# Attention solve and state products in fp32 without operand splits, with changed planner costs and offsets, in a fused attention and two-MoE kernel

## The chip, the cores and the metric

The kernel runs on one core of one Trainium2 chip. The metric is device time in microseconds (us); the median of several executions counts. A profile of one execution shows each engine: PE (TensorE matmuls; PEld is its weight loads), DVE (VectorE), ACT (ScalarE), POOL (GpSimd) and SP, which issues the DMAs.

## What is computed

A linear attention with a state of 40 x 40 per head (batch 4, 8 heads, 768 steps), then two feed-forward layers over its output, 3072 tokens of width 320 and 2048 hidden units:

```python
for t in range(S):
    y[:, :, t] = np.einsum('bhd,bhde->bhe', rt, state)
    Sa = np.einsum('bhde,bhe->bhd', state, at)
    state_decay = state * wt[:, :, None, :] - np.einsum('bhd,bhe->bhde', Sa, bt)
    state = state_decay + np.einsum('bhd,bhe->bhde', vt, kt)
x = attn_out.transpose(0, 2, 1, 3).reshape(B * S, H * D)
h = x @ w_in;    x = (h * np.cos(h)) @ w_out                        # first MoE
h = x @ w_in2;   out = (h * np.clip(h + 3, 0, 6) / 6) @ w_out2      # second MoE
```

## The kernel before, in words

The 768 steps are cut into 12 chunks of 64. A unit is one chunk of one batch entry, all 8 heads: 48 units. All matmuls of the MoE take f16 operands, each number split into a high and a low f16 part, and three products (high-high, high-low, low-high) are added in PSUM. The attention does the same with its operands before the change.

The functions of a unit, in order: `pA` loads a, r, b, k (tile `raw`) and the decays (`pip`); `pB` multiplies them and splits the result into `KBs` and `ARs`; `pT` transposes these by DMA into `KBT` and `ART`; `pC` multiplies them and masks the result (`LN`), whose upper 64 rows are split into `NT`; `pL` stores the lower 64 rows to DRAM. Per chunk, `iL` to `iE` solve 32 triangular systems: `iB` does 31 steps of two DVE instructions, `iC` and `iC1` split the result `Th` and write it through DRAM into `TT` and `Lt`, `iD` and `iE` fill the remaining block with fp32 matmuls (PSUM tile `q`). Then, per unit again: `cL` and `cV` load v and split it into `FS`; `cU` makes the right-hand side u (products of the state `ST` and of `NT` with `FS`), split into `uh` and `uls` (in `S8a`); `cA` applies the solution `TT` to u and splits the result into the lower rows of `FS`; `cAT` transposes `FS` by DMA into `FT`; `cG` multiplies it with `ART`, masks the result (`gm`) and splits it into the two `GF` tiles; `cF` makes output rows and the new state from `GF`, `E` (a copy of `KBs`) and `Srep` in one PSUM tile; `cS` decays the state `S8a`; `cST` transposes it by DMA; `cXT` transposes the output rows into `x1T`. PSUM tiles of cU, cA, cG and cF share one ring of two (`t`).

The MoE (`mA`, `mB`) runs per chunk in eight steps of two hidden blocks each: 256 matmuls into `h` for both layers together, ACT and DVE make the nonlinearity in `s` and split it into `ghl`, and 192 matmuls go into `acc`. The first MoE of a chunk needs the output rows `x1T` of that chunk's four units.

The order is not the program's. The class `Plan` records every instruction with a cost, a list scheduler replays them with a model of engines and DMA, and emits in the order that it finds; `TUNE` holds an offset of priority for each function and instruction, `SLACK`, `AHEAD` and `MARGIN` hold limits of the scheduler, `T_C` and `D_C` say at what due time a chunk's units are recorded and how far apart. An operation recorded on `either` goes to DVE or POOL, a copy to DVE or ACT, as the scheduler chooses. All compute is recorded by one helper, so nearly all rows of the profile have line L419 (L415 for copies that the scheduler put on ACT): tile names tell them apart. All DMAs but two are issued in SP's queue.

Of the kernel before, what the change touches and what calls it, by code (L numbers as in the profile page):

```python
# [43 lines left out]
T_P, D_P, T_I, D_I, T_C, D_C, T_M2, T_WM, LAG = 48.0, 2.0, 36.0, 7.0, 26.05, 2.1, 8, 150, 2  # L44
# [4 lines left out]
    "decay_const": (406, -4, -216, 2, (69, -5)),  # L49
    "decay0": (0, 509, 274, 0, (1, 42, -5, -44, -13, -34, -127, -64, -11, 116, -48, -99, 17, -40, -43, 12, -192,  # L50
        -141, -67, -15, -3, 6, -4, 32, -39, -1, -6, -10, 7, 22, -66, -28, -2, -6, 10, -7, -48)),
    "consts": (97, -153, -168, 11, (-19, 91, 1, -32, -33, 38, 4, -23, 79, 145, -9, 10, -75, 14, 4, 6, 11, -12, -35)),
    "consts1": (-254, 100, 347, 0, (-14,)),
    "consts2": (60, 417, 197, 0, (-11, -4, -48)),
    "pA": (0, 51, -99, 0, (-1, 41)),
    "pB": (0, -16, -1, 39, (0, 0, -1, 0, 0, 0, 1)),
    "pT": (-1, 70, -30, 0, (2,)),
    "pC": (-20, -1, -45, 0, (0, 2, -8, 14)),
    "pL": (1, 5, 467, 0, (-1,)),
    "rest": (124, -153, -38, 17, (-10, -2)),  # L60
    "dsq0": (-68, 293, -36, 0, (18,)),
    "chunk_decay": (-5, 51, -56, 118, (-27, 37, 3, 51)),
    "iL": (2, 22, -1287, 19, (-27, 0, -88, 35)),
    "iA": (61, -507, 208, 0, (-7, -5, -31, -12, 139)),
    "iB": (0, 0, 0, 0, (-3,)),
    "cL": (-1, 110, -26, 13, (6,)),
    "iC": (-7, -28, 23, 4, (-1, -26, -32, -81, 0, -14, 0, -10)),
    "iC1": (-4, -59, -2, 0, (89, 12, -13, -75, 13, -72, -11, -157)),
    "iD": (2, 577, 43, 51, (0, -1)),
    "cV": (1, -46, 12, 6, (-7, -3, 1)),  # L70
    "iE": (-209, 177, -297, 0, (-83, -39, 22)),
    "cU": (0, -1, -193, 0, (4, 0, -1)),
    "cA": (0, 17, -2, 0, (0, -53, 1, 3)),
    "cAT": (-74, 88, -241, 0, (-60,)),
    "cD": (-18, 7, -10, 82, (-13,)),
    "cG": (-2, -8, 9, 21, (-28, 0, -11, -7, 20, -2)),
    "cF": (-13, 1, 0, 173, (-19, 0, 0, 6, 4, 4, 6, 0, 0, -3)),
    "cXT": (-45, -151, 140, 0, (1,)),
    "cST": (5, -4, -19, 35, (2, 2, -5, -2)),
    "ld_w0": (173, -410, -126, 30, (-10,)),  # L80
    "prep_w0": (-22, 276, 9, 0, (-4, -11, 0, -2, -8, -15)),
    "decay1": (-11, 149, -9, 0, (34, 172, -8, 22, 15, -25, 42, 35, -39, 258, -75, -41, -47, -2, -30, -30, -20, -15,
        -5, 1, 0, 27, -12, -44, -6, 150, 248, 12, -9, 19, -14, -101, 9, -13, -6, -87, -23, -31)),
    "dsq1": (346, 63, -151, 0, ()),
    "decay2": (0, 274, -154, 112, (54, 240, -12, 6, 1, 0, -8, -5, 0, 38, -28, 146, -22, 23, -8, 0, -68, -32, -17,
        -7, -18, 2, 0, -52, -1, 0, 38, -19, 0, -15, 18, 6, -12, -64, -23, -31, -52, 17)),
    "cS": (-20, 1, -253, 85, (24,)),
    "dsq2": (-106, -198, -1, 0, (11,)),
    "ld_w1": (-21, 475, 315, 0, ()),
    "prep_w1": (-8, 423, 309, 0, (2, 0, -20, 0, 28, 0, 7)),  # L90
    "mA0": (0, 0, 0, 0, (0, 3, 0, 0, 12)),
    "mB0": (2, 0, 2, 0, (0, 0, 0, 0, 14, 3, 174, 12, 19, -114, 0, -170, -24, 44)),
    "mT": (373, -89, -145, 287, (-14,)),
    "mA1": (0, 8, 11, 165, (0, 26)),
    "mB1": (6, 0, 0, 0, (0, 0, 0, 5, 93, -96)),
    "mO": (-15, -533, -33, 0, (0, -4)),
    "wmax0": (-50, 365, 603, 74, (-17,)),
    "wmax1": (-49, 1, -147, 82, (4,)),
    "wcol": (-50, 302, -353, 190, (-20, -7, 0, -170, 60, -60, 105)),
    "flags": (153, -38, 4, 0, (-83, -72, 51, 21, 31, -14, 76, 60, 30, -72, 81, -15, -68, -54, -25, 111, -3, -24,  # L100
        -19, 131, -91, -99, 96, -71, 64, -111)),
# [3 lines left out]
SLACK, AHEAD, MARGIN = [132, 0, 20, 0, 383], [0, 150, 70, 54], [422, 48, 296, 22]  # L105
RING = {"raw": 2560, "KBT": 2048, "LN": 2048, "v": 1280, "uh": 640, "FT": 2048, "gm": 2048, "pd": 2560, "xy": 1280,
        "wst": 2048, "wx": 1024, "s": 2048, "xs2": 1536, "ghl": 2048, "E": 1280, "ART": 2048, "NT": 1152}
# [28 lines left out]
POOL_GAIN = 0.25  # L136
# [3 lines left out]
class Plan:  # L140
# [9 lines left out]
    def cover(self, ap):  # L150
# [6 lines left out]
        key = (off, tuple(dims), es)  # L157
# [51 lines left out]
    def rec(self, attr, eng, name, a, kw):  # L209
# [10 lines left out]
        if name.startswith("dma"):  # L220
# [6 lines left out]
            if name == "dma_start":  # L227
                run = _run(outs[0], ins[0])
                dma = by / 360.0 * (2 if run < 512 else 1)
            else:  # L230
                r, w = ins[0].shape[0], by // 2 // ins[0].shape[0]
                dma = w / 128 * 112 * r / 128
                c = 1244.0 if r == 128 and w >= 1024 else 1175.0
        elif eng == "PE":
            c = max(n / 2.4 + 2.5, 28.0)
            shape = tuple(32 if x <= 32 else 64 if x <= 64 else 128 for x in (ins[0].shape[0], _free(ins[0])))
        elif eng in ("DVE", "ANY"):
            c = 70 + n * 1.042
            es = max(mybir.dt.size(x.dtype) for x in outs + ins)
            if name == "tensor_copy":  # L240
                c = 70 + n * (0.26 if es == 2 else 0.52)
            elif name == "tensor_scalar":
                c = 70 + n * 0.52
            elif name == "reciprocal":
                c = 70 + n * 6.3
            if any(_free(x) == 1 for x in ins):
                c += 60
# [20 lines left out]
        else:  # L268
            o = dict(eng=eng, c=c, alt=cp if eng in ALTS else None, dma=dma, deps=set(), prio=self.prio, calls=[],
                     grp=(self.group, outs[0].tensor.name), i=i, port=False, shape=FULL)  # L270
# [4 lines left out]

            o["port"] = name not in ("memset", "tensor_reduce", "reciprocal") and all(getattr(x.tensor, "_space", None) != PSUM for x in ins)
# [6 lines left out]
    def order(self):  # L283
# [38 lines left out]
        start = [0] * n  # L322
        gone = set()
# [38 lines left out]
        while evs:  # L362
# [14 lines left out]
            for e in sorted(touched):  # L377
# [7 lines left out]
                if e < 4 and AHEAD[e] > 0:  # L385
                    lim = 100 * t + c * AHEAD[e]
                    if any(100 * ready_t[u] < lim and pr[u] < pr[i] - 400 * MARGIN[e] for u in soon[e]):
                        continue
                gone.add(i)
# [36 lines left out]
def label(g):  # L426
# [7 lines left out]
    elif ev[0] in "pc" and ev in ("pA", "pB", "pT", "pC", "pL", "cL", "cV", "cU", "cA", "cAT", "cD", "cG", "cS", "cF", "cXT", "cST"):  # L434
# [14 lines left out]
def _free(ap):  # L449
# [3 lines left out]
    return n  # L453

# [15 lines left out]
def kernel(  # L470
# [43 lines left out]
    cvec = big.tile([128, 4], F32, name="cvec")  # L514
# [5 lines left out]
    for nm, k in (("x", NU), ("o1", 2 * NC), ("dec", 2 * NG), ("raw", NU), ("fs", NU), ("T", 2 * NC), ("wc", 16),  # L520
# [7 lines left out]
    TTp = big.tile([128, NH * C + 64], F16, name="TT")  # L528
    TT = TTp[:, 0:NH * C].rearrange("p (h t) -> p h t", h=NH)
    FSs = [big.tile([128, H, 128], F16, name=f"FS{i}") for i in range(2)]  # L530
    GFt = [big.tile([128, H * (C + D) + 24], F16, name=f"GF{i}") for i in range(2)]
    GFh, GFl = (t[:, 0:H * (C + D)].rearrange("p (h e) -> p h e", h=H) for t in GFt)
# [6 lines left out]
    uls = S8a[0:64, 384:544].bitcast(F16).rearrange("p (h e) -> p h e", h=H)  # L539
# [5 lines left out]
    tmp = big.tile([128, 136], F32, name="tmp")  # L545
# [10 lines left out]
    Tm = [dr.tile([64, NH, 32], F32, name=f"Tm{i}") for i in range(2)]  # L556
    Thl = [dr.tile([2, C, NH, C], F16, name=f"Thl{i}") for i in range(2)]
# [26 lines left out]
    def square(src, p0, p1_, n, nm, i, o=None):  # L584
# [3 lines left out]
        if len(src.shape) == 3:  # L588
            o = o.rearrange("p (a b) -> p a b", b=src.shape[2])
# [3 lines left out]
    def consts():  # L593
        nc.sync.dma_start(out=mskL, in_=cst[0])
        nc.sync.dma_start(out=mskG, in_=cst[1])
# [873 lines left out]
```

## Time and profile before

| | us |
|---|---|
| median of 3 runs | 1272.9 (1268.25 to 1284.62) |
| the profiled execution | 1271.3 |
| its span, first to last instruction | 1269.4 |
| DVE busy in it | 1067.0 (84%) |
| PE busy | 910.1 (72%) |
| ACT busy | 792.8 (62%) |
| POOL busy | 180.4 (14%) |

Busy time is the union of an engine's instructions. A matmul row lasts from its start to its modelled end and overlaps the next ones, so the distance between two starts, not the row's length, tells what PE spends on one. Idle time of an engine counts only where the engine sets the end.

### The profile page before, as it was taken

The numbers are of one execution on the slowest core, as the hardware profiler recorded it, in microseconds if no ns is written. First come the engines' busy times: TensorE is split into PE (matmuls) and PEld (weight loads), VectorE is DVE, ScalarE is ACT, GpSimd is POOL, SyncE is SP. The second block draws the span as 40 slices with busy tenths as digits, with TensorE's granted clock in tenths as the row PEclk, the third lists the DMA queues.
The fourth block names the chain that finished last, engine by engine and source line by source line (L and its number), as shares of the span: only waits on it lengthen the run. The fifth ranks groups of instructions, "written<-read, shape, count | busy, mean of one in ns | idle before, by whom it ended". The sixth has DMA issues, their size and how long they took to land.

```text
span 1269.4 us, 29683 instructions
## 1 busy us (share of the span) xinstructions
PE 910.1 (72%) x11378; PEld 732.8 (58%) x11378; DVE 1067.0 (84%) x2434; ACT 792.8 (62%) x1642; POOL 180.4 (14%) x206
## 2 busy tenths in 40 slices
PE   0010033571668889699899898988999899999995
PEld 0000023561457668577777676766777777778874
DVE  8999999889989988869989799698796997967543
ACT  1664358485678667657676577686766866645352
POOL 2322111123423110101000010010120100100000
PEclk9999999795679899789999899899898999999998
DMA  6997478775787584776767748868477674532010
GB/s 204 244 186 177 107 225 151 159 162 124 149 171 148 108 156 102 134 144 103 130 143 135 142 83 151 148 113 155 103 126 150 115 134 93 94 63 46 11 24 14
DMA packets 474362, 162.65 MB, mean 128 GB/s; under 512 B 446789, under 2 KB 456049, under 8 KB 473826
## 3 DMA queue, kind: packets, MB, share of 16 engines
q1 hardware_dynamic: 473922, 160.00, 62.6%
q8 instruction: 91, 1.49, 0.5%
q10 hardware_dynamic: 288, 0.67, 0.2%
q14 instruction: 61, 0.50, 0.1%
HBM read 80.10 MB, written 25.61 MB: 83 GB/s over the span
## 4 chain that ended last, share of the span: by engine, by line
DVE 42%; PE 23%; DMA 11%; ACT 8%; issue 6%; SPq 3%; POOL 0%; DVEq 0%; ACTq 0%; POOLq 0%
PE acc L419 9%; PE h L419 8%; DVE Tt L419 6%; DVE tmp L419 5%; DVE S8a L419 4%; DVE ghl L419 4%; DVE wout L419 4%; PE q L419 4%; DVE s L419 3%; SPq L419 3%; DMA Lt<-Tm 2%; DVE win L419 2%; PE t L419 2%; DVE FS L419 2%; DVE GF L419 2%
## 5 line engine op out<-in xcount | busy, mean ns | idle before, releaser
L419 PE MATMUL acc<-wout,ghl 128*128 128x320 f16 x2304 | 371.8, 309 | 36.7 <-DVE ghl L419 29.6
L419 PEld LDWEIGHTS <-win 128*128 128x128 f16 x3328 | 312.1, 101 | 74.3 <-issue 27.6
L419 PEld LDWEIGHTS <-ghl 128*128 128x128 f16 x2304 | 217.1, 100 | 122.2 <-DVE ghl L419 35.1
L419 PE MATMUL h<-x1T,win 128*128 128x256 f16 (+1 forms) x1664 | 192.9, 275 | 25.4 <-DVE s L419 17.5
L419 ACT ACTIVATE s<-h,cvec 128x512 f32<-128x512 f32 x192 | 130.4, 680 | 119.4 <-PE h L419 81.8
L419 PE MATMUL h<-x2T,win 128*128 128x256 f16 (+1 forms) x1664 | 187.0, 267 | 0.0
L419 DVE TENSOR_TENSOR ghl<-s,ghl 128x512 f16<-128x512 f32 x182 | 127.6, 703 | 8.7 <-ACT ghl L415 5.2
L419 PE MATMUL p<-ART,KBT 120*128 120x64 f16 x384 | 21.4, 204 | 124.1 <-DMA ART<-ARs 73.7
L419 DVE TENSOR_TENSOR tmp<-Tt,Lt 128x126 f32<-128x126 f32 (+22 forms) x372 | 104.9, 282 | 6.5 <-DMA Lt<-Ls 3.3
L419 DVE TENSOR_TENSOR Tt<-Tt,tmp 128x126 f32<-128x126 f32 (+22 forms) x372 | 103.6, 279 | 3.6
L415 ACT ACTIVATE ghl<-s 128x512 f16<-128x512 f32 x127 | 79.3, 625 | 34.7 <-DVE s L419 27.3
L419 DVE SCALAR_TENSOR_TENSOR s<-h,s 128x512 f32<-128x512 f32 x96 | 65.7, 686 | 38.0 <-ACT s L419 37.5
L419 DVE SCALAR_TENSOR_TENSOR s<-s,h 128x512 f32<-128x512 f32 x96 | 65.2, 680 | 33.6 <-ACT s L419 33.2
L419 PEld LDWEIGHTS <-KBT 120*128 120x128 f16 x384 | 18.7, 104 | 127.7 <-DMA KBT<-KBs 84.7
L419 PE MATMUL t<-E,GF 128*128 128x40 f16 x1152 | 46.1, 184 | 40.1 <-DVE GF L419 32.3
L419 PE MATMUL q<-Lt,Tt 32*32 32x32 f32 x768 | 32.9, 203 | 49.3 <-DMA Lt<-Tm 49.3
L419 PEld LDWEIGHTS <-GF 128*128 128x128 f16 x1152 | 38.7, 99 | 49.1 <-DVE GF L419 34.5
L419 POOL TENSOR_TENSOR wout<-wout 128x512 int32<-128x512 int32 (+1 forms) x28 | 50.2, 1802 | 103.4 <-ACT wout L419 73.2
L419 PEld LDWEIGHTS q<-Lt,Tt 32*32 32x32 f32 x768 | 30.1, 118 | 53.5 <-issue 35.9
L419 PE MATMUL t<-FS,NT 128*128 128x40 f16 x768 | 36.7, 183 | 22.2 <-DVE FS L419 12.4
L419 POOL TENSOR_TENSOR S8a<-S8a,pd 40x320 f32<-40x320 f32 x23 | 25.7, 1123 | 176.0 <-DMA pd<-Ds 175.6
L419 PEld LDWEIGHTS <-ART 120*64 120x64 f16 (+1 forms) x704 | 43.9, 106 | 6.7 <-issue 4.4
(157 smaller groups left out, 1764.1 us busy)
## 6 DMA issues: line engine op xcount, KB each, us to landing
raw<-in_arbk_dram SPq DMA_DIRECT2D x46, 320.0 KB
v<-in_vv_dram SPq DMA_DIRECT2D x96, 80.0 KB
pip<-Dec SPq DMA_DIRECT2D x46, 160.0 KB
wout<-in_moe_w_in_dram SPq DMA_DIRECT2D x12, 512.0 KB
Ls<-LN SPq DMA_DIRECT2D x48, 128.0 KB
Lt<-Ls SPq DMA_DIRECT2D x48, 128.0 KB
TT<-Thl SPq DMA_DIRECT2D x12, 512.0 KB
wstat<-in_moe_w_out_dram SPq DMA_DIRECT2D x10, 512.0 KB
```

The lines of the kernel that those rows point to most:

```text
L415: self.nc.scalar.activation(func=AF.Copy, **kw)
L419: getattr(getattr(self.nc, attr), name)(*a, **kw)
```

## The change

The two f16 parts of an operand are dropped in four places, and the products take fp32 tiles: in `cU` the masked `LN` (now kept in six buffers, its lower half no longer stored as `NT`) with v; in `cA` the solution `TT` (fp32, two halves of 64 partitions) with `u32`; in `cF` the masked result and the vectors in `GFs` (fp32, two buffers) with `E`, which holds the product `bk` itself. v is loaded straight into `GFs`, and one cast and one subtraction over 128 rows make `FS` after `cA`. The products of `cU` with the state use only the first 64 columns of `ART`. `pB` makes its product in two instructions, and the upper decay rows come by a DMA in `pA` instead of a copy. The solve stores fp32 (`Tf`, two DMAs instead of four; `Tm` only half). Scaling by the decay and the split of the state work on pairs of units. In the planner, a key of its overlap cache has the partition count too, DMAs, fp32 matmuls, scans and operands at another start partition get other costs, `D_C` goes from 2.1 to 3.8, and all offsets are new.

```diff
-T_P, D_P, T_I, D_I, T_C, D_C, T_M2, T_WM, LAG = 48.0, 2.0, 36.0, 7.0, 26.05, 2.1, 8, 150, 2
+T_P, D_P, T_I, D_I, T_C, D_C, T_M2, T_WM, LAG = 48.0, 2.0, 36.0, 7.0, 26.05, 3.8, 8, 150, 2
...
-                dma = by / 360.0 * (2 if run < 512 else 1)
+                run = min(run, 20480)
+                dma = by / run * (9 + run * 0.045) / 16
...
+            if ins[0].dtype == F32:
+                c = max(4 * n / 2.4, 40.0 + 0.6 * _free(ins[0]))
...
+                if e in (1, 2):
+                    c, was[e] = c + max(o["off"], was[e]), o["off"]
...
         ldq.dma_start(out=pip[0:64].rearrange("p h x e -> p h (x e)"), in_=dec(n).rearrange("h t x e -> t h (x e)"))
+        ldq.dma_start(out=pip[64:128, :, 1], in_=dec(n)[:, :, 1].rearrange("h t e -> t h e"))
...
-        nc.either.tensor_copy(out=pip[64:128, :, 1], in_=pip[0:64, :, 1])
-        rf = raw.rearrange("p h x e -> p (h x e)")
-        nc.either.tensor_tensor(out=rf, in0=rf, in1=pip.rearrange("p h x e -> p (h x e)"), op=ALU.mult)
+        bk = E_t[n] = pE.tile([128, H, D], F32, tag="E", name="E")
+        nc.either.tensor_tensor(out=bk, in0=raw[:, :, 1], in1=pip[:, :, 1], op=ALU.mult)
+        nc.either.tensor_tensor(out=raw[:, :, 0], in0=raw[:, :, 0], in1=pip[:, :, 0], op=ALU.mult)
...
-        E_t[n] = pE.tile([128, H, 2 * D], F16, tag="E", name="E")
-        nc.either.tensor_copy(out=E_t[n], in_=kb[:, :, 0:2 * D])
...
-        ntp = pN.tile([128, H * C + 64], F16, tag="NT", name="NT")
-        nt = ntp[:, 0:H * C].rearrange("p (h t) -> p h t", h=H)
-        nc.either.tensor_copy(out=nt[64:128], in_=ln[64:128])
-        dp("nt", E_NT).tensor_tensor(out=nt[0:64], in0=ln[64:128], in1=nt[64:128], op=ALU.subtract)
...
-        nc.sync.dma_start(out=Tm[i][0:32].rearrange("(t k) h s -> (k h) t s", k=2), in_=Tn)
-        nc.sync.dma_start(out=Tm[i][32:64].rearrange("(a r) h t -> (r h) a t", r=2), in_=Th[64:128])
-        nc.sync.dma_start(out=TM, in_=Tm[i])
-        nc.sync.dma_start(out=TT, in_=Thl[i].rearrange("x s h t -> (x s) h t"))
+            nc.sync.dma_start(out=Tf[i][32 * k:32 * k + 32, :, 32 * k:32 * k + 32].rearrange("(a r) h t -> (r h) a t", r=2),
+                              in_=Th[64 * k:64 * k + 64])
+        nc.sync.dma_start(out=Tm[i].rearrange("(t k) h s -> (k h) t s", k=2), in_=Tn)
+        nc.sync.dma_start(out=TM[0:32], in_=Tm[i])
+        nc.sync.dma_start(out=TM[32:64], in_=Tf[i][32:64, :, 32:64])
+        for g in range(2):
+            nc.sync.dma_start(out=TT[64 * g:64 * g + 64], in_=Tf[i][:, 16 * g:16 * g + 16])
...
-        nc.vector.scalar_tensor_tensor(out=TT[64:96, hs, 32:64], in0=qv[32:64], scalar=ISC, in1=TT[0:32, hs, 32:64],
-                                       op0=ALU.mult, op1=ALU.subtract)
...
-        ldq.dma_start(out=v[64:128], in_=vv[n])
-        ldq.dma_start(out=v[0:64], in_=vv[n])
-        V_t[n] = v
+        ldq.dma_start(out=GFs[n % 2][64:128, :, C:C + D], in_=hde(vv[n]))
...
+        if c > 0:
+            for h in range(H):
+                nc.tensor.matmul(uv[:, h, :], art[:120, h, 0:C], stt[:120, h, 0:D], start=(h == 0), stop=False)
         for h in range(H):
-            w = nt[:, h * C:h * C + 128]
-            if c > 0:
-                nc.tensor.matmul(uv[:, h, :], art[:120, h, :], stt[:120, h, 0:D], start=True, stop=False)
-            nc.tensor.matmul(uv[:, h, :], w, fs[:, h, 0:40], start=(c == 0), stop=False)
-            nc.tensor.matmul(uv[:, h, :], w, fs[:, h, 40:80], start=False, stop=True)
...
+            nc.tensor.matmul(uv[:, h, :], ln[64:128, h, :], gf[64:128, h, C:C + D], start=(c == 0 and h == 0),
+                             stop=(h == H - 1))
+        nc.scalar.activation(out=u32[p:p + 64], in_=uv, func=AF.Copy, scale=ISC)
...
         for h in range(H):
-            nc.tensor.matmul(av[:, h, :], tt[0:64, h * C:h * C + 128], ul[:, h, :], start=(h == 0), stop=False)
-        for h in range(H):
-            nc.tensor.matmul(av[:, h, :], tt[:, h * C:h * C + 128], uh[:, h, :], start=False, stop=(h == H - 1))
...
+            nc.tensor.matmul(av[:, h, :], TT[p:p + 64, q + h, :], u32[p:p + 64, h, :], start=(h == 0), stop=(h == H - 1))
+        nc.scalar.activation(out=gf[0:64, :, C:C + D], in_=av, func=AF.Copy, scale=-ISC2)
...
-        gm = p1.tile([128, H, C], F32, tag="gm", name="gm")
...
-        gh, gl = GFh, GFl
-        nc.either.tensor_copy(out=gh[:, :, 0:C], in_=gm)
-        nc.either.tensor_copy(out=gh[:, :, C:C + D], in_=fs[:, :, 0:40])
-        nc.either.tensor_copy(out=gl[:, :, C:C + D], in_=fs[:, :, 40:80])
-        dp("gl", E_GL).tensor_tensor(out=gl[:, :, 0:C], in0=gm, in1=gh[:, :, 0:C], op=ALU.subtract)
...
         for h in range(H):
-            nc.tensor.matmul(fv[:, h, :], gl[h], kb[:, h, 0:40], start=(h == 0), stop=False)
+            nc.tensor.matmul(fv[0:R, h, :], gf[:, h, :], bk[:, h, :], start=(h == 0), stop=(c == 0 and h == H - 1))
         if c > 0:
             for h in range(H):
                 nc.tensor.matmul(fv[0:64, h, :], art[:120, h, C:2 * C], Srep[b][:, h, :], start=False, stop=False)
-        for h in range(H):
-            nc.tensor.matmul(fv[:, h, :], gh[h], kb[:, h, 40:80], start=False, stop=False)
-            nc.tensor.matmul(fv[:, h, :], gh[h], kb[:, h, 0:40], start=False, stop=(h == H - 1))
+
+            nc.tensor.matmul(fv[0:R, H - 1, 0:1], gf[:, H - 1, :], zero, start=False, stop=True)
```

## Rows read from the trace of the kernel before

**Rows 1.** Windows by stage: us; busy of PE, PEld, DVE, ACT, POOL; clock, DMA
```profile
0.00:228.00 228.00, 27.97 (x524) 24.69 (x525) 212.68 (x442) 120.67 (x220) 54.74 (x70) 1.00 0.76 183
228.00:528.00 300.00, 207.73 (x2783) 168.16 (x2781) 270.16 (x585) 205.71 (x421) 71.67 (x59) 0.83 0.68 141
528.00:1024.00 496.00, 451.35 (x5565) 359.77 (x5565) 425.15 (x1037) 345.28 (x740) 47.77 (x68) 0.95 0.71 130
1024.00:1168.00 144.00, 135.57 (x1764) 110.90 (x1763) 115.98 (x288) 85.87 (x191) 6.22 (x9) 1.00 0.47 86
```

**Rows 2.** DVE groups: operation out<-in, shapes, count | busy us, mean ns | idle before
```profile
L419 DVE TENSOR_TENSOR raw<-raw,pip 128x640 f32<-128x640 f32 x45 | 38.4, 854 | 4.4 <-DMA TT<-Thl 3.3 <-DMA raw<-in_arbk_dram 0.8
...
L419 DVE TENSOR_TENSOR GF<-gm,GF 128x512 f16<-128x512 f32 x48 | 35.0, 729 | 0.0
L419 DVE TENSOR_TENSOR NT<-LN,NT 64x512 f16<-64x512 f32 x48 | 33.5, 698 | 2.1 <-ACT NT L415 0.5
...
L419 DVE SCALAR_TENSOR_TENSOR FS<-v,FS 128x320 f16<-128x320 f32 x48 | 23.2, 483 | 1.1 <-ACT FS L419 0.7
L419 DVE SCALAR_TENSOR_TENSOR S8a<-t,uh 64x320 f16<-64x320 f32 x48 | 23.0, 478 | 3.4 <-ACT uh L419 2.9
...
L419 DVE SCALAR_TENSOR_TENSOR TT<-q,TT 32x512 f16<-32x512 f32 x24 | 16.4, 685 | 25.8 <-ACT TT L419 25.6
...
L419 DVE CAST GF<-gm 128x512 f16<-128x512 f32 x24 | 10.7, 444 | 0.1
...
L419 DVE COPY GF<-FS 128x320 f16<-128x320 f16 x32 | 8.8, 276 | 0.0
```

**Rows 3.** ACT groups, the same view
```profile
L415 ACT ACTIVATE E<-KBs 128x640 f16<-128x640 f16 x46 | 33.7, 732 | 9.0 <-DVE KBs L419 7.9 <-PE t L419 0.8
...
L415 ACT ACTIVATE GF<-FS 128x320 f16<-128x320 f16 x64 | 29.4, 459 | 7.6 <-DVE FS L419 3.9 <-PE t L419 3.5
...
L415 ACT ACTIVATE uh<-uh 64x320 f16<-64x320 f16 x45 | 21.1, 468 | 1.2
```

**Rows 4.** Timeline of PE, 732 to 746 us: start, duration, operation, count
```profile
738.50 0.36 PE L419 MATMUL t<-E,GF 128*128 128x40 f16 x8
738.79 0.43 PE L419 MATMUL t<-Srep,ART 120*64 120x40 f16 x8
739.15 0.57 PE L419 MATMUL t<-E,GF 128*128 128x40 f16 x16
739.57 0.18 PE L419 MATMUL t<-ST,ART 120*128 120x40 f16 x1
...
740.17 1.91 PE L419 MATMUL h<-x2T,win 128*128 128x256 f16 x16
742.00 0.39 PE L419 MATMUL t<-ART,FT 120*128 120x64 f16 x8
742.32 0.37 PE L419 MATMUL t<-S8a,TT 64*128 64x40 f16 x8
...
742.84 1.38 PE L419 MATMUL acc<-wout,ghl 128*128 128x320 f16 x9
744.06 1.91 PE L419 MATMUL h<-x2T,win 128*128 128x256 f16 x16
745.81 0.36 PE L419 MATMUL t<-E,GF 128*128 128x40 f16 x8
```

**Rows 5.** Timeline of PE at two fp32 groups [idle before, releaser]
```profile
717.75 1.19 PE L419 MATMUL q<-Lt,Tt 32*32 32x32 f32 x32 [2.61 <-DMA Lt<-Tm]
...
1235.38 0.23 PE L419 MATMUL t<-one,acc 128*72 128x1 f32 x2
```

**Rows 6.** The page's DMA queue row: packets, MB, share of 16 engines
```profile
q1 hardware_dynamic: 473922, 160.00, 62.6%
```

**Rows 7.** Windows after the first fp32 block, columns as in rows 1
```profile
720.00:726.70 6.70, 6.70 (x56) 4.61 (x53) 3.09 (x5) 2.26 (x4) 0.00 (x0) 0.52 0.57 140
726.70:734.00 7.30, 7.30 (x117) 5.91 (x117) 4.84 (x15) 5.83 (x12) 0.00 (x0) 1.00 0.55 119
```

## The prediction: what the change does to the time

> **What bounds the kernel.** I began with the busy time of each engine by stage [rows 1]. The stages are cut where a chunk's first MoE 1 matmul starts: 0 to 228 us is the start, then come chunks 0 to 2 (three periods of 100 us), chunks 3 to 8 (six of 82.7), chunks 9 and 10 (two of 72) and the tail. The attention of chunk 0 is done in the start, of 1 to 3 in the second stage, of 4 to 9 in the third, of 10 and 11 in the fourth: 4, 12, 24 and 8 units. In the start DVE is busy 212.68 of 228 us (93%), then 270.16 of 300 (90%): DVE bounds both, beside DMA engines at 0.76 and 0.68. In the third stage DVE has 425.15 of 496 us (86%) and PE 451.35 (91%). In the fourth DVE falls to 81% and the period to 72 us.
>
> PE's busy rows overlap, so I took its occupancy from distances of starts in the timeline [rows 4]: nine acc matmuls take 744.06 - 742.84 = 1.22 us, 0.136 each, and sixteen h matmuls 745.81 - 744.06 = 1.75: 0.109. A chunk has 192 and 256 of them: 26.1 + 27.9 = 54.0 us. Attention on PE, per unit: cF runs from 738.50 to 739.57 (1.07), cU to 740.17 (0.60), cA from 742.32 to 742.84 (0.52), cG 0.32 before it; pC is taken as cG, having its shapes. Eight matmuls at 0.029 make 0.23 of cG's 0.32: the other 0.09 is the change of tile shape into cA. The fp32 products of the solve come in four blocks per chunk of 32 instructions, 1.19 us to the last one's end [rows 5]: 1.1 each. So 54.0 + 4 x (1.07 + 0.60 + 0.52 + 0.64) + 4.5 = 69.8 us of PE work per chunk. Of 82.7 us 12.9 are idle or lost to the clock; of 72 only about 3. PE alone would thus allow 70 us; DVE's fuller queue holds the third stage 10 us above the fourth's idle.
>
> **What leaves DVE and ACT.** DVE loses the split of the masked G (GF TENSOR_TENSOR 35.0, CAST 10.7, COPY 8.8), the low half of N (33.5), the first split of v (23.2), the low half of u (23.0) and of the solve's block (16.4) [rows 2]: 150.6 us. The multiplication by the decay goes from one 640-element instruction of 854 ns to two of 320, at 483 each by the FS row: +0.11 x 48 = +5. Net 145 us of 1067, 3.0 per unit, 12 per chunk; smaller casts (of T, NT, pip) leave too and are not counted. The second split of FS stays. ACT loses at least the E copy, the FS copies and the copy of u, 33.7 + 29.4 + 21.1 = 84 us [rows 3]; it is below 70% busy in every stage [rows 1], so this only gives the plan room for casts. In cA, ACT now makes one copy of 320 elements more before FS is cast (the nearest row of that size has 483 ns), and behind it wait ACT's Square and SP's transpose of FS; cF in turn loses GF's cast and subtraction (444 and 729 ns [rows 2]) ahead of its products, so the unit's chain grows no longer. DVE's 25.6 us of idle before TT [rows 2] go too: cA then waits for ACT's copy alone, and next for PE's second block of the solve, which is as late as before.
>
> **What PE pays.** The products of N with v (cU), of the solution with u (cA) and of G with E (cF) become fp32: per unit 16 + 16 + 24 f16 instructions go, and 8 + 8 + 8 fp32 products come, each of two instructions if they are built as the solve's, 32 for the 16 products of a block [rows 5]. There an instruction takes (1.19 - 0.18) / 31 = 0.033 us (a lone one lasts 0.18, the ST row of rows 4) with 32 weight and 32 moving columns. Now there are 40 moving and 64 (cU, cA) or 104 (cF) weight columns, shown nowhere. Lower end: 0.033 again, 0.066 a product. Upper end, if the time goes with the weight columns: 0.132 and 0.215. The one fp32 product with wide weights (72 columns) takes its two instructions in 0.23 us [rows 5]: at most 0.05 apart, nearer the lower end. So I scale by the moving columns: 0.083, and 0.088 for cF.
>
> Per unit after: the products with the state lose half their weight columns and cost what Srep's eight do [rows 4], 0.36 less one change of shape: 0.27; cU and cA 0.66 each; cF 0.70 + 0.27 for Srep + 0.09 for the closing product with zero; and seven changes of shape where there were three, at the 0.09 seen before cA, 0.63. Sum 3.28, against 1.07 + 0.60 + 0.52 + 0.09 = 2.28: **+1.0 us per unit, 4.0 per chunk, 48 in all.** The ends give 2.8 (+0.5) and 5.2 (+2.95).
>
> A rule of the Trainium skill speaks against this: TensorE: Matmul & The Clock Gate, LDWEIGHTS, gives a load the time of its columns at 1.2 GHz, and Weight-path perf modes says that the fast load is not for fp32. By it a product would take 0.107 or 0.173, a unit 4.4 us, and the total would be about 1270. The rows don't bear that rate out for 64 f16 columns: Srep's instructions stand 0.27 / 8 = 0.034 apart, where the rule has 0.053; for fp32 no row here settles it.
>
> **DMA, queues and order.** pip gets a third load per unit, v one load instead of two; the solve's stores and loads go from nine to eight per chunk; the issues in SP's queue stay level, and nothing is moved past them. In pieces: pip adds 512 of 160 bytes per unit, v goes from 128 of 1,280 to 512 of 160, the solve saves about 2,000 per chunk: about +18,000 on 473,922, 4%. At q1's 62.6% [rows 6] that is 2 to 3 points of share: hidden in the third stage, not surely in the start, so the lower gain there. The stall before the solve (2.61 us of PE, for Lt [rows 5]) stays: T still goes through DRAM. The planner's new costs and offsets change only the order and who makes a cast; no row prices that. I take 0; both signs are among the rivals.
>
> **The sum.** Start: DVE loses 4 x 3.0 and N for some seven units ahead, 17 us; at its 93% share 18. Ends 0 (all hidden behind DMA and the chain) and -18; taken -12. Second stage: 12 x 3.0 = 36, at 90% share 40; ends 0 and -40; taken -30, as DVE is the fuller engine there, but the clock of 0.83 and a PE with 10 us more work hold some back. Third: 69.8 + 4.0 + 4.5 = 78.3 us, with an idle between the fourth stage's 3 and 6, since DVE then has 73 of 100 us; 4.4 x 6 = -26. Fourth: 8 x 1.0 = +8, -2 of idle: +6. Tail: no attention, 0. Together -62: 1269.4 - 62 + 1.9 around the span (1271.3 is the profiled run) = 1209; the median shown is 1.6 above that run: **1211 us.**
>
> **Rivals.**
> *Deeper.* The start and second stage give all of DVE's time (-18, -40), products cost the lower end and idle falls to 3: third stage 69.8 + 2.2 + 3 = 75.0 (-46), fourth 0: 1169. For it: DVE's 93 and 90%. Against: 0.76 of DMA. 0.18.
> *Hidden.* DMA and the chain of chunk 0 set the first two stages: 0, 0, -26, +6: 1253, the border of 2%. For it: DMA's shares. Against: DVE rests only 15 us in 228. 0.09.
> *The products cost the upper end,* weight loads bounding them and PE everything: third stage 69.8 + 11.8 + 4.5 = 86.1, +20; fourth +22, second -5, start -8: 1302, slower by 2.3%. It decides from +2.0 us a unit, where the third stage gains nothing. Against: at most 0.05 at 72 columns. 0.10, of which 0.04 at the end itself. The rule of the Trainium skill told above would land in this case, near its point of decision.
> *The clock.* At 717.75 PE has waited 2.61 us and runs an fp32 block, and from 720 to 726.7 the granted clock is 0.52, the 1.2 GHz level for nearly all of it [rows 5, 7]. Such a stretch costs 3.2 us. If each unit's fp32 groups brought one: 13 per chunk, third stage 78.3 + 13 (+52), fourth 6 + 26 (+32), second about 0, start -12: 1345. Slower by 2% from 27 such stretches on (62 + 25 us, over 3.2). Against: 726.7 to 734 holds two more fp32 blocks and runs at 1.00 [rows 7]: the wait, not the type, stands before the fall. 0.06.
>
> **How the numbers follow.** The forecast has 0.57, with a range of its own of 1180 to 1240. 1160 to 1260 leaves out the upper price, the clock and some 0.04 below 1160. Faster by over 2% (about what a measurement here can tell; below 1247): forecast, deeper and nearly half of hidden, 0.79; within 2%: the rest of hidden and 0.06 of the upper price, 0.11; slower: 0.04 of that and the clock, 0.10.
>
> **What would show it.** DVE's busy time near 920 us and no GF, NT or TT splits; fp32 rows of LN, TT and GF with starts near 0.042 us apart (0.066 and 0.107 would be the upper price); chunks 3 to 8 at 78 us with PE work of 74; fourth stage near 75 each; clock not below 0.95 in the third. I am wrong if the third stage keeps 82 us while DVE's share falls, or if the start grows: then order or DMA, not DVE, bounds.

## The result and the profile after

The changed kernel takes 1286.6 us in the median, the kernel before 1268.6 on the same chip: a ratio of 1.0131, with a 95% interval of 1.0106 to 1.0157. It is 1.3% slower, where 1211 against 1272.9 us, 4.9% faster, was forecast. Medians are of all executions, while the ratios leave out single ones in the chip's slower state (here one of 18, 1539.45 us). The profiled execution has 1282.93 us and a span of 1281.2.

The page of the kernel after, busy time (share of the span) by engine, and the chain that ended last:

```profile
PE 1036.0 (81%) x11082; PEld 855.8 (67%) x11082; DVE 938.2 (73%) x2183; ACT 648.6 (51%) x1378; POOL 120.2 (9%) x147
...
PE 67%; DVE 14%; DMA 7%; SPq 3%; issue 2%; ACT 2%; POOL 0%; ACTq 0%; DVEq 0%; POOLq 0%
PE h L429 23%; PE acc L429 21%; PE t L429 19%; PE q L429 4%; DVE Tt L429 4%; SPq L429 3%; DVE wout L429 2%; DMA Lt<-Tm 2%; DMA wout<-in_moe_w_in_dram 2%; DVE win L429 1%; DMA out_dram<-s 1%; DVE acc L429 1%; DVE ghl L429 1%; DVE s L429 1%; DVE x2T L429 1%
```

The same chain in the page of before:

```profile
DVE 42%; PE 23%; DMA 11%; ACT 8%; issue 6%; SPq 3%; POOL 0%; DVEq 0%; ACTq 0%; POOLq 0%
```

The bound has changed over from DVE to PE, and 19% of the span's chain is now products of cU, cA, cG and cF, which go into the PSUM tile `t` (2% before).

Windows of the kernel after, cut as in [rows 1] where a chunk's first MoE 1 matmul starts (columns as there, with GB/s last):

```profile
0.00:235.00 235.00, 45.05 (x455) 41.15 (x456) 214.60 (x435) 107.64 (x202) 62.74 (x58) 1.00 0.77 196
235.00:501.00 266.00, 231.73 (x2720) 194.57 (x2720) 209.54 (x485) 163.12 (x354) 45.62 (x48) 0.88 0.70 142
501.00:1015.00 514.00, 503.64 (x5400) 413.59 (x5399) 362.77 (x916) 277.29 (x611) 10.82 (x36) 0.95 0.61 124
1015.00:1180.00 165.00, 163.62 (x1748) 135.10 (x1746) 103.31 (x253) 69.14 (x148) 1.01 (x5) 0.96 0.36 72
1180.00:1282.00 102.00, 91.97 (x767) 71.39 (x765) 47.95 (x97) 31.41 (x64) 0.00 (x0) 0.97 0.08 19
```

Against [rows 1] the stages changed by +7, -34, +18, +21 and 0 us. DVE fell from 425.15 to 362.77 us in the third stage, as it should have. PE rose from 451.35 to 503.64, 98% of a stage that is longer than before. The time that DVE gave up became waiting, as DVE's own waits show, before (L419) and after (L429; us in total, times, longest):

```profile
DVE s L419 <- ACT s L419: 70.7, 53, 4.1
DVE xy L419 <- PE t L419: 2.2, 4, 0.7
```
```profile
DVE s L429 <- ACT s L429: 144.7, 87, 5.7
DVE xy L429 <- PE t L429: 53.2, 47, 2.9
```

`xy` is what DVE makes of cF's product: after the change DVE waits for it in 47 of 48 units, before it did in 4. The cause stands in PE's groups (busy, mean ns of one | idle before):

```profile
L429 PE MATMUL t<-E,GF 128*104 128x40 f32 x768 | 85.6, 275 | 17.9 <-DVE GF L429 17.6 <-ACT wout L429 0.3
L429 PE MATMUL t<-Tt,TT 64*64 64x40 f32 x768 | 63.7, 247 | 7.4 <-ACT Tt L429 6.6 <-issue 0.7
L429 PE MATMUL t<-GF,LN 64*64 64x40 f32 x768 | 59.4, 239 | 7.8 <-DVE LN L429 6.7 <-ACT S8a L425 1.1
```

Each is 768 instructions for 384 products, two for a product, as forecast. What one costs is read from starts. The timeline of PE at the place that answers [rows 4]:

```profile
713.73 1.57 PE L429 MATMUL t<-E,GF 128*104 128x40 f32 x16
715.23 0.43 PE L429 MATMUL t<-Srep,ART 120*64 120x40 f16 x8
715.59 0.34 PE L429 MATMUL t<-cvec,GF 128*104 128x1 f32 x2
715.79 0.57 PE L429 MATMUL acc<-wout,ghl 128*128 128x320 f16 x3
...
720.10 0.43 PE L429 MATMUL t<-ST,ART 120*64 120x40 f16 x8
720.46 1.12 PE L429 MATMUL t<-GF,LN 64*64 64x40 f32 x16
721.51 2.54 PE L429 MATMUL t<-E,GF 128*104 128x40 f32 x16
723.99 0.62 PE L429 MATMUL t<-Srep,ART 120*64 120x40 f16 x8
...
737.15 1.12 PE L429 MATMUL t<-Tt,TT 64*64 64x40 f32 x16
738.21 1.80 PE L429 MATMUL acc<-wout,ghl 128*128 128x320 f16 x12
```

Sixteen `GF,LN` instructions take 721.51 - 720.46 = 1.05 us, 0.066 each with the change of shape among it; the sixteen of `E,GF` at 713.73 take 1.50 us, 0.094 each. The group at 721.51 takes 2.48 us: from 722 to 732 us the granted clock is 0.50, the 1.2 GHz level. Between two starts inside a group the median of the third stage is 58 ns with 64 weight columns and 92 with 104. A unit costs 2.06 (cF, to 715.79) + 1.41 (cU, from 720.10) + 1.06 (cA) = 4.53 us where it was 2.28 [rows 4]: +2.25, not +1.0.

### The profile page after: what moved, and what is told of

Its sections match the earlier page's. It is cut to its first block, busy times and chain, and to the rows that moved or that the text cites. A ratio compares the mean times of both kernels' runs of the same rounds, so it can differ in the third digit from the quotient of the medians.

```text
span 1281.2 us, 28401 instructions
## 1 busy us (share of the span) xinstructions
PE 1036.0 (81%) x11082; PEld 855.8 (67%) x11082; DVE 938.2 (73%) x2183; ACT 648.6 (51%) x1378; POOL 120.2 (9%) x147
## 4 chain that ended last, share of the span: by engine, by line
PE 67%; DVE 14%; DMA 7%; SPq 3%; issue 2%; ACT 2%; POOL 0%; ACTq 0%; DVEq 0%; POOLq 0%
PE h L429 23%; PE acc L429 21%; PE t L429 19%; PE q L429 4%; DVE Tt L429 4%; SPq L429 3%; DVE wout L429 2%; DMA Lt<-Tm 2%; DMA wout<-in_moe_w_in_dram 2%; DVE win L429 1%; DMA out_dram<-s 1%; DVE acc L429 1%; DVE ghl L429 1%; DVE s L429 1%; DVE x2T L429 1%
## 5 line engine op out<-in xcount | busy, mean ns | idle before, releaser
L429 PE MATMUL acc<-wout,ghl 128*128 128x320 f16 x2304 | 376.4, 310 | 7.6 <-DVE ghl L429 4.2
L429 PEld LDWEIGHTS <-win 128*128 128x128 f16 x3328 | 313.0, 101 | 73.3 <-issue 21.3
L429 PEld LDWEIGHTS <-ghl 128*128 128x128 f16 x2304 | 219.8, 101 | 93.1 <-DVE ghl L429 6.4
L429 ACT ACTIVATE s<-h,cvec 128x512 f32<-128x512 f32 x192 | 131.1, 684 | 196.6 <-PE h L429 158.5
L429 PE MATMUL h<-x1T,win 128*128 128x256 f16 (+1 forms) x1664 | 186.8, 269 | 23.3 <-DVE s L429 17.3
L429 PE MATMUL h<-x2T,win 128*128 128x256 f16 (+1 forms) x1664 | 199.2, 277 | 0.0
L429 DVE TENSOR_TENSOR ghl<-s,ghl 128x512 f16<-128x512 f32 x189 | 131.2, 695 | 12.8 <-ACT ghl L425 6.0
L429 PE MATMUL p<-ART,KBT 120*128 120x64 f16 x384 | 21.2, 203 | 144.3 <-DMA KBT<-KBs 135.3
L429 DVE SCALAR_TENSOR_TENSOR s<-h,s 128x512 f32<-128x512 f32 x96 | 65.9, 689 | 87.5 <-ACT s L429 86.7
L429 PEld LDWEIGHTS <-KBT 120*128 120x128 f16 x384 | 18.1, 104 | 148.5 <-DMA KBT<-KBs 137.3
L429 DVE SCALAR_TENSOR_TENSOR s<-s,h 128x512 f32<-128x512 f32 x96 | 65.8, 685 | 59.2 <-ACT s L429 58.0
L429 DVE TENSOR_TENSOR Tt<-Tt 128x126 f32<-128x126 f32 (+22 forms) x372 | 100.9, 271 | 4.2
L429 PE MATMUL t<-E,GF 128*104 128x40 f32 x768 | 85.6, 275 | 17.9 <-DVE GF L429 17.6
L429 DVE TENSOR_TENSOR Tt<-Tt,Lt 128x126 f32<-128x126 f32 (+22 forms) x372 | 95.4, 257 | 3.6
L429 PEld LDWEIGHTS t<-E,GF 128*104 128x104 f32 x768 | 83.2, 188 | 19.7 <-DVE GF L429 11.6
L429 PE MATMUL t<-Tt,TT 64*64 64x40 f32 x768 | 63.7, 247 | 7.4 <-ACT Tt L429 6.6
L429 PEld LDWEIGHTS t<-Tt,TT 64*64 64x64 f32 x768 | 57.7, 156 | 15.8 <-ACT Tt L429 7.3
L429 PE MATMUL t<-GF,LN 64*64 64x40 f32 x768 | 59.4, 239 | 7.8 <-DVE LN L429 6.7
L429 DVE SCALAR_TENSOR_TENSOR xy<-t,cvec,pd 104x320 f32<-104x320 f32 (+1 forms) x48 | 26.4, 550 | 53.2 <-PE t L429 53.2
L429 PEld LDWEIGHTS t<-GF,LN 64*64 64x64 f32 x768 | 53.6, 147 | 9.7 <-DVE LN L429 6.9
L429 POOL TENSOR_TENSOR wout<-wout 128x512 int32<-128x512 int32 (+2 forms) x29 | 49.0, 1695 | 96.7 <-ACT wout L429 62.2
```

What stands on the lines that cost most here:

```text
L429: getattr(getattr(self.nc, attr), name)(*a, **kw)
```

## The experiments

Theory P, formed from these rows: DVE's relief is real, but an fp32 product costs PE 1.4 times (64 weight columns) to 2.1 times (104) what was forecast, and PE takes back all of it. Its rivals: the new plan or the wider distance of the units loses the time; the chain of a unit does; VectorE and DMA do, in the start. The runs come from several chips, on which the kernel before has 1268.6 to 1273.6 us, so they are compared by their ratios to it; 0.01 of ratio is 12.7 us.

**Cheap products in the same order (e1).** Same instructions on DVE and ACT, same order on every engine; the three kinds of products read the upper 16 bits of each operand through a view, so that part of the result has fewer bits. The edit of cF, with the view (cU and cA in the same way):

```diff
+    def hb(t):
+        n = t.shape[1]
+        return t.rearrange("p a b -> p (a b)").bitcast(BF16).rearrange("p (a b x) -> p a b x", a=n, x=2)[:, :, :, 1]
...
-                nc.tensor.matmul(fv[0:R, h, :], gf[:, h, :], bk[:, h, :], ...
+                nc.tensor.matmul(fv[0:R, h, :], hb(gf)[:, h, :], hb(bk)[:, h, :], ...
```

> The changed kernel in its own order, instruction for instruction; only the products of cU, cA and cF read the upper 16 bits of the same fp32 tiles (a bf16 view), so each is one instruction instead of two and loads 16-bit weights. Left out: the lower 16 bits of these operands. Theory P (the fp32 products cost too much of PE): 24 products per unit fall from 0.116 and 0.183 us to 0.03 to 0.09, at least 1.9 us per unit; PE, which now ends the chain, has 7.6 us less per chunk: chunks 3 to 8 at 77 to 79 us instead of 85.7, the total 1200 to 1225. Theory O (the new order loses, not the products): the period stays above 83 and the total above 1265.

Measured: 1191.0 us, a ratio to before of 0.9376 (0.9348 to 0.9404): below Theory P's range, and far from Theory O's. Its windows:

```profile
0.00:224.00 224.00, 25.56 (x357) 22.03 (x358) 213.40 (x435) 106.48 (x201) 62.43 (x58) 1.00 0.80 203
224.00:472.00 248.00, 199.91 (x2412) 160.48 (x2409) 208.44 (x484) 163.57 (x356) 47.80 (x49) 0.86 0.76 153
472.00:933.00 461.00, 430.47 (x4805) 342.26 (x4806) 357.54 (x917) 271.04 (x609) 10.83 (x36) 0.98 0.70 137
933.00:1080.00 147.00, 141.74 (x1556) 112.69 (x1555) 103.17 (x256) 69.59 (x152) 1.01 (x5) 0.98 0.44 83
1080.00:1182.00 102.00, 91.48 (x764) 71.09 (x761) 47.57 (x96) 31.43 (x64) 0.00 (x0) 0.97 0.08 18
```

DVE's columns are those of the changed kernel; PE's third stage has 73 us less. From stage to stage the price of the products is 235 - 224 = 11, 266 - 248 = 18, 514 - 461 = 53, 165 - 147 = 18 and 0: 100 us of span, more than the whole miss. This is the price over single 16-bit products, of which there are 24 a unit where the kernel before has 56 f16 ones: so the 6.2% that e1 gains on before are not the removed splits alone, but these, the fewer products and the new plan together.

**The price by itself (e4).** In a single execution, behind the last matmul of the changed kernel, stand seven groups of 16 fp32 products each, over weight columns and moving columns:

```diff
+        for q, (M, N) in enumerate(((32, 40), (64, 40), (104, 40), (128, 40), (64, 20), (104, 20), (104, 80))):
+            hp = ps_h.tile([128, 512], F32, tag="h", name="bench")
+            for k in range(16):
+                rnc.tensor.matmul(hp[0:M, 0:N], bx[:, 8 * k:8 * k + M], by[:, 8 * k:8 * k + N], start=True, stop=True)
```

> The changed kernel with seven groups of 16 fp32 products behind its last matmul, on idle data, 128 rows: weight columns x moving columns 32x40, 64x40, 104x40, 128x40, 64x20, 104x20, 104x80. Nothing is left out. By weight columns: starts of the two instructions of a product 0.032, 0.058, 0.092, 0.112 us apart for 32 to 128 columns, and the same 0.058 and 0.092 with 20 moving columns, 0.092 with 80. By moving columns (the forecast): 0.04 for all with 40, half with 20, 0.08 with 80.

Windows from the first start of a group to just past a later one of its instructions, for 32, 64 and 104 weight columns with 40 moving, then 64 and 104 with 20 moving:

```profile
1285.04:1286.14 1.10, 1.10 (x31) 1.10 (x31) 0.00 (x0) 0.44 (x1) 0.00 (x0) 1.00 0.30 75
1286.30:1288.08 1.78, 1.78 (x34) 1.77 (x31) 0.18 (x1) 0.00 (x0) 0.00 (x0) 1.00 0.56 137
1288.29:1291.06 2.77, 2.77 (x32) 2.77 (x31) 0.18 (x1) 0.00 (x0) 0.00 (x0) 1.00 0.02 6
1298.12:1301.34 3.22, 3.22 (x31) 3.22 (x31) 0.18 (x1) 0.00 (x0) 0.00 (x0) 0.50 0.00 0
1301.65:1306.87 5.22, 5.22 (x31) 5.22 (x31) 0.18 (x1) 0.00 (x0) 0.00 (x0) 0.50 0.00 0
```

With 31 weight loads in each, hence 30 distances, an instruction costs 37, 59 and 92 ns at the clock's upper level and 107 and 174 at the lower. At the lower level 104 columns take 174 ns with 20 moving columns and, read from single starts, 173 with 80. So the price of these fp32 products goes with the weight columns, and between 20 and 80 moving columns not with those. For the weight columns a rule of the Trainium skill has the same: TensorE: Matmul & The Clock Gate, LDWEIGHTS, gives a load its columns over 1.2 GHz, 27, 53 and 87 ns here. The rows at the upper level agree with it, with some 5 to 10 ns added.

**Which product (e5, e6).** e5 has the view for the closing product cF alone, e6 for cU and cA alone ("alpha" is cA's result).

> The changed kernel in its own recorded order, but the closing product alone (E,GF and the one-column product behind it) reads the upper 16 bits of its operands; the products of u and of alpha stay in fp32. What is computed is changed in that part: the closing product has fewer bits. Theory P (the price of an fp32 product on TensorE sets the loss, and every product weighs what its starts weigh): in the third stage of the changed kernel the closing product took 1.82 us a unit of starts against 0.63 with 16 bits, so 1.19 us x 48 = 57 us of TensorE; the run in which all three read 16 bits turned 129 us of starts into 96 us of time, three quarters, so 1287 - 43 = 1244 us (1235 to 1253). Rival L (the loss sits in the chain of one unit, where u, alpha, G and the closing product follow each other, and only the products ahead of alpha are on it): under 10 us, 1277 or more. Rival S (one of the two kinds alone carries it, since the other fills gaps of TensorE): 1195 or 1280.

> The mirror of the run before: the products of u (GF,LN) and alpha (Tt,TT) read the upper 16 bits, the closing product stays in fp32. Again fewer bits in that part. Theory P: 2.23 us a unit of starts against 0.72, so 1.50 us x 48 = 72 us of TensorE, three quarters of it 54 us: 1233 us (1223 to 1243). Rival L (the chain of a unit, where u and alpha come first): most of the 96 us, 1200 or less. Rival S: 1195 or 1280. If the two gains add up to about 96 us, the parts weigh by their starts alone.

Measured: e5 1225.2 us, 0.9606 (0.9507 to 0.9705), some 67 us under the changed kernel's ratio; e6 1217.6, 0.954 (0.9463 to 0.9617), some 75 under it. Their third stages:

```profile
483.00:962.00 479.00, 462.54 (x5188) 376.55 (x5187) 358.21 (x913) 272.46 (x608) 10.84 (x36) 0.98 0.69 131
```
```profile
487.00:963.00 476.00, 459.95 (x5025) 373.43 (x5026) 360.44 (x918) 273.96 (x612) 10.80 (x36) 0.97 0.69 133
```

Both expectations were too small: they counted three quarters of the starts saved (57 and 72 us), and about all of it came. The gains add to some 140, but together (e1) they give 96. In chunks of the third stage PE's busy time falls by 6.8, 7.3 and 12.2 us (e5, e6, e1), the period by 5.8, 6.3 and 8.8: what is taken first from a PE that is 98% busy comes back nearly whole, what is taken later less so, and PE waits longer for other engines. Its waits for `s` and `FT`, in the changed kernel and in e1:

```profile
PE h L429 <- DVE s L429: 17.3, 12, 8.3
PE t L429 <- DMA FT<-FS: 8.6, 3, 5.2
```
```profile
PE h L429 <- DVE s L429: 24.4, 16, 8.7
PE t L429 <- DMA FT<-FS: 22.3, 14, 7.4
```

That rules out both rivals: neither the chain alone nor one kind alone carries the loss.

**The plan (e2, e3).** e2 computes as the changed kernel with the old costs, offsets, limits and distance; with the close distance the load of the second next unit's v comes ahead of cF in half of the units, so that part of cF's operand is another unit's. The instructions are the same, but a wait is left out, so e2's time is if anything too short. e3 computes as the kernel before, with the new costs, offsets, limits and distance.

The distance in e2, beside the table of offsets and the lines of costs of the diff, which go back too (in e3 the same lines go the other way):

```diff
-T_P, D_P, T_I, D_I, T_C, D_C, T_M2, T_WM, LAG = 48.0, 2.0, 36.0, 7.0, 26.05, 3.8, 8, 150, 2
+T_P, D_P, T_I, D_I, T_C, D_C, T_M2, T_WM, LAG = 48.0, 2.0, 36.0, 7.0, 26.05, 2.1, 8, 150, 2
...
-POOL_GAIN = 0.34
+POOL_GAIN = 0.25
```

> The computation of the changed kernel with the costs, offsets, limits and D_C of the kernel before (the offsets were found for other instructions, so some loss comes with it). Theory P: still bound by PE, chunks 3 to 8 at 85 us or more, total 1280 to 1330. Theory O: the old order suits; total below 1250, and the start shorter than 235 us.

> The computation of the kernel before with the new costs, offsets, limits and D_C (the entry of cV, which the change drops, keeps its old offsets). Theory P: the order costs or gains little: 1255 to 1300, DVE as busy as before (about 1067 us). Theory O: slower than before by what the changed kernel loses and by the DVE time that it saves: 1320 or more.

Measured: e2 1316.6 us, 1.0321 (1.0286 to 1.0356); e3 1256.4, 0.987 (0.9842 to 0.9898). The plan is not what loses: by the ratios it gains some 16 us with splits and 24 without. Under one and the same plan, going from splits to fp32 costs 33 us (the new one) or 41 (the old one). e3 keeps all the bits and is 1.3% faster than before. Its windows up to the tail:

```profile
0.00:236.00 236.00, 31.09 (x569) 27.31 (x570) 223.25 (x458) 122.25 (x222) 65.66 (x71) 1.00 0.78 186
236.00:521.00 285.00, 205.27 (x2737) 165.31 (x2736) 256.52 (x568) 203.84 (x413) 67.83 (x62) 0.84 0.69 143
521.00:1008.00 487.00, 438.45 (x5567) 351.77 (x5568) 428.56 (x1036) 345.77 (x724) 63.88 (x85) 0.98 0.72 131
1008.00:1153.00 145.00, 137.76 (x1751) 111.88 (x1750) 115.79 (x287) 85.45 (x188) 7.35 (x12) 0.98 0.46 85
```

**The planner's price (e9), and new offsets (e10, e11).** The planner priced these products at 78 and 102 ns where the chip takes 116 and 184.

```diff
-                c = max(4 * n / 2.4, 40.0 + 0.6 * _free(ins[0]))
+                c = 2 * (_free(ins[0]) / 1.2 + 5.0)
```

> The changed kernel with one line of its planner altered: an fp32 product is priced at 2 x (weight columns / 1.2 + 5) ns, as the run of bare products measured it (117 and 183 ns for 64 and 104 columns, where the changed planner has 78 and 102); offsets as they are. Theory P (TensorE itself is too slow with these products, in any order): within 1% of the changed kernel, 1275 to 1300 us, since the same products run. Rival M (the planner's wrong price put work into bad places, and that is the loss): 1260 or less.

> The run before, with the planner's offsets, slacks and limits searched anew for that price by the planner's own end time: its end falls from 1180.7 to 1165.2 us. The kernel with splits under the new planner had an end of 1152.6 by the same sums and 1256 measured, 104 more, so Theory P expects 1165 + 104 = 1269 us (1255 to 1285): the fp32 products can't get under the kernel before by more than 1% by order alone. Rival M: 1240 or less.

> The kernel with operand splits everywhere, as before the change, under the new planner, with its offsets searched in the same way and for as long: the planner's end falls from 1152.6 to 1118.5 us. Theory P (the splits had the cheaper TensorE, and VectorE has room left for a better order): 1118 + 104 = 1222 us (1205 to 1245), 40 to 50 us under the fp32 kernel searched alike. Rival V (VectorE, 85% busy, leaves no room, and a planner's end gained there isn't met on the chip): 1250 or more.

Measured: e9 1276.4 us, 1.0025 (0.9991 to 1.0059); e10 1277.7, 1.0025 (0.9989 to 1.0061); e11 1284.0, 1.007 (1.0037 to 1.0102). The right price is worth 1.1%, some 13 us: that is most of the 17 us lost against the kernel before, but less than half of the 33 lost against splits under the same plan (e3), and nothing of the 4.9% forecast comes with it. Under all four plans (the old one, the new one, e9's and e10's) the fp32 products end at the time of before or above it, as Theory P has it. The search is a miss. e10's 15 us of the planner's end came out as nothing, and e11's 34 us as a loss of 25 against e3. Its windows show the place:

```profile
0.00:278.00 278.00, 29.32 (x540) 25.95 (x541) 257.03 (x509) 139.92 (x250) 68.95 (x75) 1.00 0.77 182
278.00:541.00 263.00, 193.13 (x2754) 158.50 (x2752) 238.49 (x545) 194.48 (x406) 66.53 (x59) 0.87 0.70 139
541.00:1029.00 488.00, 446.59 (x5598) 356.99 (x5596) 420.84 (x1033) 343.23 (x740) 60.51 (x85) 0.97 0.73 132
```

The third stage is as long as e3's (488 and 487 us), but the first MoE matmul starts at 278 us where e3 has 236, and the second stage gives back only 22 of these 42. So in these runs the planner's own end did not tell how good an order is, and they say nothing on what the best plan for either form is.

**Splitting cF alone again (e7, e8, e12).** cF, and the G, v and keys that it reads, go back to f16 splits; cU, cA and the solve stay in fp32. For want of space the two buffers of v become one.

```diff
-            nc.tensor.matmul(fv[0:R, h, :], gf[:, h, :], bk[:, h, :], ...
+            nc.tensor.matmul(fv[:, h, :], gl[h], kb[:, h, 0:40], start=(h == 0), stop=False)
...
+            nc.tensor.matmul(fv[:, h, :], gh[h], kb[:, h, 40:80], start=False, stop=False)
+            nc.tensor.matmul(fv[:, h, :], gh[h], kb[:, h, 0:40], start=False, stop=(h == H - 1))
```

> Only the state/output product goes back to f16 operand splits (24 products with 128-column weights, and the copies and subtractions that split G, v and the keys on VectorE, ScalarE and GpSimd); u, alpha and the solve stay as changed, with the new planner and offsets. Theory P: the closing product falls from 1.82 us a unit to about 0.9 (24 starts of about 32 ns and the change of shape), so 0.9 x 48 = 44 us of TensorE, of which three quarters, 33 us, come back; VectorE gets some 40 to 60 us of splits again, which in the third stage (363 of 514 us busy) find idle time but lengthen a unit's chain: 1255 us (1240 to 1270), near the 1256 of the kernel that has splits everywhere under the new planner. Rival V (VectorE is the bound again as soon as splits come back): not better than that kernel, 1265 or more. Rival F (the splits are free now): 1240 or less.

> As the run before, with the distance of a chunk's units at the old 2.1 in place of 3.8 (the product's v lies in a buffer of its own here, so the closer units don't meet). Theory D (the wider distance was needed for the buffers and costs time, since the first chunk's four units spread from 30 us to 71 us): 5 to 15 us less than the run before, most of it in the start. Rival (a planner sorts by ready times anyway, and denser units jam VectorE): no better, or up to 30 us worse, as the changed kernel under the old plan was.

> The kernel in which the state/output product alone is split again, whose order, made with offsets meant for another list of operations, gave 1302 us: now with the right fp32 price and offsets searched in the same way: the planner's end falls from 1202.3 to 1149.0. Theory O (that run was slow since the offsets didn't fit its operations, not since the split costs more than it gives): 1149 + 104 = 1253 us (1235 to 1270), between the fp32 kernel and the split kernel searched alike. Rival C (the split of this product itself costs VectorE and the chain of a unit more than TensorE gets back): 1285 or more.

Measured: e7 1301.6 us, 1.0195 (1.0114 to 1.0276); e8 1275.1, 0.9985 (0.9937 to 1.0033); e12 1293.9, 1.0132 (1.0077 to 1.0187). In e7 PE's work falls as expected (986.9 us busy, 49 less), yet the time does not: its interval overlaps that of the changed kernel (1.0106 to 1.0157) and reaches above it. So Theory P and Rival F failed. Rival V's number came (1265 or more), but not its cause: in the third stage DVE is busy 394 of 520 us, PE 479.

```profile
529.00:1049.00 520.00, 479.32 (x5583) 386.70 (x5582) 394.42 (x972) 292.94 (x607) 16.23 (x39) 0.95 0.69 123
```

PE's waits in e7:

```profile
PE h L429 <- DVE s L429: 34.9, 14, 10.9
PE t L429 <- DMA FT<-FS: 30.7, 8, 8.9
...
PE h L429 <- DMA x1T<-S8a: 23.0, 9, 6.8
...
PE t L429 <- DMA GV<-in_vv_dram: 10.6, 5, 5.2
```

After the change the waits for `s`, `FT` and `x1T` were 17.3, 8.6 and 6.0 us. Work left PE and waits came in its place: a unit's chain got its splits back, behind a single v (`GV`). How much of it is the order, the one buffer or the longer chain isn't settled. e8 has 26 us less, but doesn't settle it: it too has one buffer, against what its expectation says, and in 36 of 47 units the load of the next unit's v comes ahead of FS's split, which then reads another unit's v. So e8 leaves out waits (PE waits 5.1 us for `GV` where e7 has 10.6), and its 26 us don't show what the distance alone is worth. They don't come from the start, as Theory D has it: the first MoE matmul is at 242 us, in e7 at 239. In e12, whose offsets were searched, Theory O failed and Rival C's number came. This stays open; it doesn't bear on the changed kernel.

## Why the prediction was wrong, step by step

**The bound, right; what leaves DVE, right.** DVE went from 1067 to 938.2 us (near 920 forecast), and no split of G, N or T is left. The added DMA packets were 17,888, against 18,000. That the second stage gained 34 us where 30 were taken is in part luck: with cheap products it gains 52 (e1), and their price takes 18 back.

**The price of a product: the step that failed.** It was taken as 0.083 and 0.088 us, two instructions scaled by the moving columns, from the row of 72 columns [rows 5]. Measured are 0.116 and 0.184. The bounds were right (0.066 to 0.132 and 0.215), the choice between them was not. The error is in the reading of that row: it is a lone pair between other work. The weight loads (PEld) of the pair, and what PE runs behind it:

```profile
1235.25 0.28 PEld L419 LDWEIGHTS t<-one,acc 128*72 128x72 f32 x2
```
```profile
1235.48 0.70 PE L419 MATMUL acc<-wout,ghl 128*128 128x320 f16 x4
```

The first load begins 0.13 us ahead of the pair's first start (1235.38), so the 29 ns between the pair's two starts don't hold it. The next acc matmul starts 65 ns after the second one, about what e4's rows give for 72 columns between the 59 ns of 64 and the 92 of 104. In the kernel after, too, 28 of 48 closing groups have their first two starts 35 ns apart, then 85, and then 92 for each one more. A train's price can't be read from its first pair. The sum by the rule of the Trainium skill told there (TensorE: Matmul & The Clock Gate, LDWEIGHTS), 0.107 and 0.173 us and 4.4 us for a unit, was the better one: 4.53 is measured. That rule did fail for f16 with 64 columns, as the prediction said (0.032 a start here), but a rate that doesn't hold for one type was no evidence on the other.

**The third stage.** 78.3 us a chunk were forecast, 85.7 came. At the measured +2.25 a unit the same sum has 69.8 + 9.0 + 4.5 = 83.3: the price is 5.0 of the 7.4 us missed. The other 2.4 are the term of 4.5 for idle and the clock, which was too small: PE rests 514 - 503.64 us, 1.7 a chunk, and by an estimate from the granted clock of 0.95 another 4.3 a chunk are lost to the lower level. In e1 it was too small as well: 76.8 came, and with PE's work 0.3 us a unit below before (from its starts) the sum has 69.8 - 1.3 + 4.5 = 73.0.

**The start.** -12 was taken, +7 came. Three steps, read from the windows, lead there: +8 by the new plan with splits (e3 against before), -12 with the splits dropped and cheap products (e1 against e3), +11 by the price of the products (after against e1). So under the new plan the 12 us that were taken are gained, though against the kernel before e1 has only -4. The plan's share belongs to this order of steps: with fp32 under the old plan (e2) the start takes 250 us, so there the new plan gains 15. As to the price, a closing group costs 2.80 us there, 173 ns from start to start, which is the price of the lower level, and the last one ends just ahead of the first MoE matmul:

```profile
232.38 2.99 PE L429 MATMUL t<-E,GF 128*104 128x40 f32 x16
235.18 2.12 PE L429 MATMUL h<-x1T,win 128*128 128x128 f16 x18
```

The sums had no such case. The window's granted clock reads 1.00 there, but these `h` matmuls stand 107 ns apart up to 237.3 us and 56 from then on, and only there does the trace's record of the granted clock begin.

**The sign of being wrong.** The third stage kept more than 82 us while DVE's share fell, and the start grew. The prediction read that sign as order or DMA in place of DVE; it was PE.

**The plan at nothing.** Not so, and none of the four rivals held it, though the prediction says so: it is worth some 16 us with splits (e3) and 24 without (e2), a gain; its wrong price takes some 13 of it back (e9). Counting it would have moved the forecast further from the result.

**The rivals.** The one at the upper price had the mechanism, and its point of decision, +2.0 us a unit, was passed. Its numbers against the result: third stage 86.1 a chunk (85.7), fourth +22 (+21), start -8 (+7), second -5 (-34), together 1302 (1287). That 86.1 is so near is in part luck: its price was 2.8 us a chunk too high and its idle 2.4 too low. It held 0.10 and should have held most. The clock's rival fell: the third stage runs at 0.95, as before.

## What to carry to other kernels

Price an fp32 matmul with few moving columns by its weight columns, and read the price from a train of equal ones, never from the first two. Replacing three f16 products by one fp32 product, itself two instructions, was no saving on PE here: 2.28 us a unit became 4.53. It moves time from DVE to PE, so look first at how idle PE is in that stage. Don't take a planner's end time as the measure of an order: here a search that lowered it by 3% lost 2% on the chip.

## What the runs showed of the hardware beyond that

With 104 weight columns an fp32 product's price does not change between 20 and 80 moving columns (e4). For f16 it does not go with the weight columns as it does for fp32: instructions with 128 columns stand 25 ns apart in e7's closing product (16 in 0.42 us before [rows 4]), those with 64 columns 32, and fp32 ones with 104 columns 92. In e4, with nothing but fp32 products on PE, the granted clock was 1.00 for the first 6 us and 0.50 for the 20 after it, and an instruction went from 59 to 107 ns (64 columns) and from 92 to 174 (104). In e1 the third stage has 0.98 where the changed kernel has 0.95; but e9, with the same fp32 products as the changed kernel in another order, has 0.98 there too. In the start the products have the price of the lower level under a granted clock that reads 1.00, since that record begins only at 237 us: where it has no record yet, take the level from the distance of starts.
